# A state-space filter and a gated MLP in one kernel: block 1's signal transform with one split, shift taps on 32-row strips, another home for the third filter's sums, and new instruction orders

## The chip, the cores and the metric

One core of one Trainium2 chip runs the kernel. A core has five engines that run side by side and meet through semaphores: TensorE (PE in the profile, with its weight loads as PEld), VectorE (DVE), ScalarE (ACT), GpSimd (POOL) and SyncE (SP). DMA engines move data; transfers are issued from the queues of SP, POOL and ACT. The metric is the device time in microseconds (us) of one launch.

## What is computed

Batch 1, S = 2048 tokens, D = 640 channels, hidden width F = 1728, bf16 in and out.

```python
x = A_q
# A: gated long convolution, over the normalised x
k_shift = sum over t of k[token - t] * shift_k[:, t]        # 4 taps a channel
kv  = k_shift * v
y   = causal convolution of kv with ssm_k along the tokens  # by FFT of length 2 S
y   = y + kv * ssm_D
h   = x + layernorm(x) * y
# B: gated MLP
g, u = silu(layernorm(h) @ w_gate), layernorm(h) @ w_up
out = h + (g * u) @ w_down
```

## The kernel before

**Blocks.** The tokens are cut into four blocks of N = 512 (i = 0 to 3), and so is the filter ssm_k (m = 0 to 3). Each block of signal and each piece of filter is transformed on TensorE, with tables of cosines and sines (`tab`, `itab`) as the stationary operand; block i of the output is the sum over j of signal j times filter i-j, in the transformed domain, and an inverse transform. `SEQ` at L351 gives the order in which the steps are written down: P product, K third filter, W weights, F feed-forward, S signal, I inverse.

**Transforms.** There are three ways. `fulls` (L593) computes all four quarters of the spectrum by 64 matmuls. `halves` (L574) splits once: 32 matmuls in eight PSUM tiles of four, for the sums over even and over odd positions, then two VectorE operations over 2560 elements (a butterfly: difference and sum). `quads` (L611) splits twice: 16 matmuls in eight tiles of two, then four VectorE operations over 1280 elements and two over 2560. `R4X` (L363) names the blocks whose signal goes by `quads`; the filters go by `halves`. Each PSUM tile of 128 x 640 is copied to SBUF by an eviction (L455), on ScalarE or VectorE.

**The third filter.** `kfwd(2)` (L659) leaves the even half in the first half of K2r and the odd half in the buffer KO. For the filters named in `LO`, VectorE makes the difference (`kb2.0`), and the sum is a DMA that adds KO into K2r (`addto`, L570, issued by POOL; `kb2.1`). `kcomb(2)` (L677) then forms the running sum of filters 1 and 2 in R1, by one VectorE operation over 5120 elements (`kc2.s`, L687). For filters named in `KD` that sum goes by two accumulating DMAs.

**Taps.** `taps(i)` (L699) makes the four-tap shift on TensorE. k is held transposed (channels on partitions); the moving operand is `diag`, the tap weights spread on diagonals of 64 columns, so that two row halves of the array work on 64 channels each. A column group c of 128 channels takes 7 shifts x 2 halves = 14 matmuls (L734) of 64 to 256 columns. For blocks 1 to 3 the tile is evicted into XT (`ke`), and VectorE multiplies it by v (`kv`, L745): three tiles, three evictions and three products a block.

**Order.** No engine's order follows from the program text: `PLAN` (L259) lists, for each engine, the numbers of its tasks in the order in which they run, and the PSUM tile (of four, of two banks each) that each task's result takes. A task waits for the tasks whose data or buffers it needs (L192), so a task that is late holds up all that is listed behind it on its engine. Evictions and some other tasks can run on either of two engines, and the list decides.

**Names that the prediction uses.** `kf`m and `xf`i are the forward matmuls of filter m and signal i, with `e` their evictions, `kt` the transposes of a filter and `kte` their evictions; `kb`, `xb`, `yb` butterflies; `kc` running sums; `p`ji products; `iv`i.j inverse, followed by `e` eviction, `g` product with x, `m` and `s` two statistics passes on ScalarE, `v` and `r` the power -1/2 (r on POOL), `n` normalising; `ht` the DMA transposes of the result; `fg`, `fu` feed-forward matmuls (gate, up), `sg`, `su` their evictions and `mu` their product; `dn` down-projection, `rs` its eviction.

Of the kernel before, what the change touches and what calls it, by code (L numbers as in the profile page):

```python
# [50 lines left out]
class _Graph:  # L51
# [41 lines left out]
    def add(self, name, engs, fn, kind, r=(), w=(), pr=(), pw=(), skip=(), dma=False):  # L93
# [4 lines left out]
        t.opens = None  # L98
# [18 lines left out]
        for pt in pw:  # L117
            if not pt.writers:
                t.opens = pt
# [15 lines left out]
    def arrange(self, plan):  # L135
# [19 lines left out]
        for t in self.order["pe"]:  # L155
            if t.opens is not None:
                prev = last.get(t.opens.unit)
                if prev is not None:
                    t.pre = {x for x in prev.users if x.eng != "pe"}
                    t.deps.update(t.pre)  # L160
                last[t.opens.unit] = t.opens
# [21 lines left out]
    def emit(self, block):  # L183
# [29 lines left out]
        for t in self.glob:  # L213
            kn = known[t.eng]
            fill = self.fills.get(t.name)
            if fill:
                wait_for(t, t.pre | {x for x in t.deps if x.name == fill[0]})
                prog["pe"].append(lambda e, t=t, fill=fill: self.filler(e, t.opens, *fill))
# [50 lines left out]
    "act":  # L269
# [10 lines left out]
    "dve":  # L280
# [10 lines left out]
    "pool":  # L291
        "19 17 15 16 125 165 174 158 192 183 223 225 224 342 396 362 281 371 285 401 380 289 406 389 343 293 420 415 527 466 "
# [18 lines left out]
def bass_sequential_preLN__ssm_conv_h3__swiglu_ffn__prompt_kernel(  # L311
# [917 lines left out]
```

## Time and profile before

| What | Value |
|---|---|
| median of 3 runs | 259.0 us (258.26 to 259.75) |
| profiled execution, first to last instruction | 256.0 us |
| PE busy | 248.5 us (97%), 2253 matmuls |
| PEld busy | 194.7 us (76%) |
| DVE busy | 199.8 us (78%), 256 instructions |
| ACT busy | 184.6 us (72%), 302 instructions |
| POOL busy | 58.6 us (23%), 56 instructions |
| granted TensorE clock | 1.000 |
| moved by DMA | 35.29 MB |

The profiled execution's own time is its span, 256.0 us; the median of the timed runs lies 3.0 us above it, which holds what stands before the first and after the last instruction. The share of a whole span hides stages, so the slices of the page are of more use: the busy tenths of each engine in 40 slices of 6.4 us.

```profile
PE   7999997999999999999999999999999999999995
DVE  3698999999999999999999989999959534111142
ACT  2489999999996895587899789739981854526410
```

PE is busy everywhere, but the ends of its matmuls are modelled, so gaps between issues don't show there. VectorE is full from the third slice to past the middle; ScalarE is full in two stretches, the first of them where the filters and the signal of block 1 are transformed.

### The profile page before, as it was taken

What the parts mean: (1) busy time and instruction counts of PE and PEld (TensorE: products, weight loads), DVE (VectorE), ACT (ScalarE), POOL (GpSimd) and SP (SyncE); (2) the same over time, 40 slices, a digit from 0 to 9 for tenths busy, and PEclk for the clock granted to TensorE, in tenths of its full rate; (3) what the DMA queues carried; (4) which work ended last, traced back from release to release, by engine and by line L of the source; (5) the groups of instructions that cost most, each with busy time, mean ns of one, the idle gap of its engine ahead of it and who ended that gap; (6) DMA issues with size and microseconds to landing.
All of it is one profiled execution on the core that took longest, in us unless ns stands there. A gap on an engine that the chain in (4) does not pass through costs nothing.

```text
span 256.0 us, 5303 instructions
## 1 busy us (share of the span) xinstructions
PE 248.5 (97%) x2253; PEld 194.7 (76%) x2253; DVE 199.8 (78%) x256; ACT 184.6 (72%) x302; POOL 58.6 (23%) x56
## 2 busy tenths in 40 slices
PE   7999997999999999999999999999999999999995
PEld 4767773587888766888887766788886678888763
DVE  3698999999999999999999989999959534111142
ACT  2489999999996895587899789739981854526410
POOL 1001003082312053950030813334130314000000
PEclk9999999999999999999999999999999999999999
DMA  6999946787995049886956036497870142600011
GB/s 224 323 339 208 403 161 134 220 207 192 326 188 95 0 75 126 150 165 168 248 100 109 3 55 139 108 213 139 149 128 0 30 100 43 140 0 3 0 45 57
DMA packets 37620, 35.29 MB, mean 138 GB/s; under 512 B 21203, under 2 KB 32478, under 8 KB 37598
## 3 DMA queue, kind: packets, MB, share of 16 engines
q1 hardware_dynamic: 31792, 23.82, 33.2%
q0 software_dynamic: 5792, 11.14, 25.3%
q8 instruction: 17, 0.28, 0.4%
q14 instruction: 5, 0.04, 0.1%
q10 hardware_dynamic: 14, 0.01, 0.0%
HBM read 16.55 MB, written 2.62 MB: 75 GB/s over the span
## 4 chain that ended last, share of the span: by engine, by line
PE 59%; DVE 32%; DMA 4%; POOL 1%; SPq 1%; issue 1%; ACT 0%; DVEq 0%
PE ps L1032 32%; PE ps L1118 16%; DVE tt L780 9%; DVE Y L780 5%; DMA tab<-cst_tab 4%; PE ps L602 3%; PE ps L922 2%; DVE gu L1053 2%; DVE C L780 2%; DVE XH L637 2%; DVE C L564 2%; PE ps L995 2%; PE ps L622 2%; PE ps L584 2%; POOL mv L840 1%; SPq L450 1%
## 5 line engine op out<-in xcount | busy, mean ns | idle before, releaser
L1118 PE MATMUL ps<-Wd,gu 128*128 128x320 bf16 (+1 forms) x420 | 58.7, 300 | 0.0
L1118 PEld LDWEIGHTS ps<-Wd,gu 128*128 128x128 bf16 (+1 forms) x420 | 38.7, 97 | 18.4 <-issue 3.6
L780 DVE TENSOR_TENSOR tt<-XH,C 128x2560 bf16<-128x2560 bf16 (+1 forms) x31 | 47.8, 1572 | 0.6 <-ACT XH L458 0.6
L1053 DVE TENSOR_TENSOR gu<-gu,ub 128x1024 bf16<-128x1024 bf16 (+1 forms) x32 | 19.9, 621 | 26.4 <-ACT gu L1040 13.8
L1040 ACT ACTIVATE gu<-ps 128x1024 bf16<-128x1024 f32 (+1 forms) x32 | 29.4, 924 | 12.1 <-PE ps L1032 11.9
L1045 ACT ACTIVATE ub<-ps 128x1024 bf16<-128x1024 f32 x24 | 24.6, 1024 | 13.3 <-PE ps L1032 11.4
L1032 PE MATMUL ps<-hnT,GB 128*128 128x256 bf16 x280 | 34.0, 273 | 0.0
L1032 PE MATMUL ps<-hnT,UB 128*128 128x256 bf16 x280 | 33.8, 273 | 0.0
L1032 PEld LDWEIGHTS ps<-hnT,UB 128*128 128x128 bf16 x280 | 27.3, 98 | 3.4 <-ACT KO L458 0.2
L1032 PEld LDWEIGHTS ps<-hnT,GB 128*128 128x128 bf16 x280 | 27.2, 98 | 3.3
L1032 PE MATMUL ps<-hnT,GA 128*128 128x256 bf16 x240 | 28.8, 273 | 0.0
L1032 PE MATMUL ps<-hnT,UA 128*128 128x256 bf16 x240 | 28.5, 273 | 0.1
L840 POOL TENSOR_TENSOR mv<-mv,half 128x1 f32<-128x1 f32 x16 | 21.2, 1328 | 23.9 <-DVE mv L838 23.9
L1032 PEld LDWEIGHTS ps<-hnT,UA 128*128 128x128 bf16 x240 | 23.4, 98 | 3.4 <-ACT C L458 0.5
L1032 PEld LDWEIGHTS ps<-hnT,GA 128*128 128x128 bf16 x240 | 23.4, 98 | 3.2 <-DVE XH L461 0.3
L843 ACT ACTIVATE qo<-xh 128x640 bf16<-128x640 bf16 x28 | 21.0, 750 | 5.8 <-DMA xh<-in_A_q_dram 3.3
L584 PE MATMUL ps<-KT,tab 128*128 128x320 bf16 x128 | 19.8, 300 | 1.8 <-ACT K3r L458 0.7
L937 ACT ACTIVATE qo<-ps,one,st 128x640 bf16<-128x640 f32 x16 | 13.7, 887 | 9.8 <-PE ps L922 9.0
L571 POOL DMA_DIRECT2D xh<-RB x12 | 10.7, 889 | 34.4 <-DVE RB L1135 23.0
L584 PEld LDWEIGHTS ps<-KT,tab 128*128 128x128 bf16 x128 | 11.4, 98 | 8.6 <-ACT K3r L458 1.6
L840 POOL TENSOR_TENSOR st<-st,half 128x4 f32<-128x4 f32 x4 | 8.0, 1988 | 33.3 <-DVE st L835 21.5
L458 ACT ACTIVATE XH<-ps 128x640 bf16<-128x640 f32 x19 | 13.3, 736 | 1.4 <-PE ps L622 0.7
(112 smaller groups left out, 384.3 us busy)
## 6 DMA issues: line engine op xcount, KB each, us to landing
C<-US POOLq DMA_DIRECT2D x6, 640.0 KB, 6.0
kc<-in_A_ssm_k_dram SPq DMA_DIRECT2D x4, 640.0 KB, 10.3
xh<-in_A_q_dram SPq DMA_DIRECT2D x4, 640.0 KB, 5.6
out_dram<-xh SPq DMA_DIRECT2D x15, 160.0 KB, 1.9
kvo<-in_A_v_dram SPq DMA_DIRECT2D x3, 640.0 KB, 4.5
xh<-RB POOLq DMA_DIRECT2D x12, 160.0 KB, 2.9
Wd<-in_B_w_down_dram SPq DMA_DIRECT2D x1, 1280.0 KB, 7.9
C<-K3r POOLq DMA_DIRECT2D x2, 640.0 KB, 8.0
```

Of the source, the lines that this page charges most:

```text
L458: return e.activation(out=dst[1], in_=src(), func=ACTF.Copy, scale=scale)
L571: return g.add(name, "pool", lambda e, n: e.dma_start(dst, src, accum_op=ALU.add, max_dma_last_dim=4096), ("acc", 2 * int(np.prod(dst.shap ...
L584: last = e.matmul(pt.f(c, W), tab[:, f, cs, j], src[:, j, c * W:(c + 1) * W], start=(j == js[0]), stop=(j == js[1]))
L780: g.add(nm, "dve", lambda e, n_: e.tensor_tensor(out=d, in0=a, in1=b, op=op), ("sb", n * D), r=[a, b], w=[d])
L840: g.add(name + "r", "pool", lambda e, n: e.tensor_tensor(out=dst, in0=tmp, in1=hf, op=ALU.pow), ("pp", 4), r=[tmp, half[:]], w=[dst])
L843: g.add(name + "m", "act", lambda e, n: e.activation(out=junk, in_=x, func=ACTF.Identity, scale=-1.0 / D, accum_out=sm), ("aa", D, 0), r=[ ...
L937: g.add(nm + "e", "act", lambda e, n, pt=pt, q2=q2, s=s, j=j: e.activation(out=q2, in_=pt.f2(W), func=ACTF.Identity, scale=s[:, 3, j:j + 1 ...
L1032: last = e.matmul(pt.f(q // 2, 256, o=256 * (q % 2)), w[:, c, f0:f0 + P], hnT[:, c, cols], start=(c == 0), stop=(c == NC5 - 1))
L1040: g.add("sg%d.%d%d" % (i, h, gp), "act", lambda e, n, pa=pa, gv=gv, nf=nf: e.activation(out=gv, in_=pa.f(0, 256 * nf).rearrange("p (f x) - ...
L1045: g.add("su%d.%d%d" % (i, h, gp), "act", lambda e, n, pb=pb: e.activation(out=ub[:].rearrange("p b x -> p (b x)"), in_=pb.f(0, 1024), func ...
L1053: g.add("mu%d.%d%d" % (i, h, gp), "dve", lambda e, n, gv=gv, ubv=ubv: e.tensor_tensor(out=gv, in0=gv, in1=ubv, op=ALU.mult), ("sb", 256 * ...
L1118: last = e.matmul(pt.f(c, W), gu[k, fb, col(i, j)], Wd[k, fb, c * W:(c + 1) * W], start=st, stop=sp)
```

## The change

Seven parts of it act; the rest renames (`BNH` to `BNT`), makes room for choices that are not taken (`KOT`, `DV`, several buffers KO at one address), or lets a matmul task open two PSUM tiles (`opens` becomes a list).

- `R4X` loses block 1: `xfwd(1)` goes by `halves`.
- `KD` gains 2: `kc2.s` becomes two DMAs issued by POOL, `kc2.0` and `kc2.1`.
- `LO` loses ('k', 2): `kb2.1` becomes a VectorE operation over 2560 elements.
- Taps of blocks 1 to 3: column groups 0 to 3 together as one task on four strips of 32 rows, 28 matmuls of 32 to 128 columns for each group, in two PSUM tiles with two evictions (`a`, `b`); the fifth group as before. One product `kv` of 2048 elements takes the place of two of 1024.
- Five evictions early in the kernel run on VectorE that ran on ScalarE (kte2.1, kte3.1, ke1.4, kf2e.010, kf2e.001; kte0.1 in place of kte0.0), and kf0e.011 goes to ScalarE.
- TensorE's order: of block 0's signal one tile, not two, stands ahead of filter 0; all of xf1 and most of filter 3 stand ahead of the first feed-forward task.
- Queues: on SP `itab` stands behind the loads of block 1's x and v, and block 2's v behind the first output; on POOL kc2.0 and kc2.1 stand between iv0.1r and iv0.2r.

The choices:

```diff
     LF = (0, 1, 2, 3)
     SA = ()
     DA = ((1,2),(1,3),(2,3),(3,3))
-    KD = (3,)
+    KD = (2,3)
     DD = (2,)
-    LO = (('k',2),('k',3),('x',3))
+    DV = ()
+    LO = (('k',3),('x',3))
     RD = (0,1,2)
     KS = (1,)
     TS = ((3,3),)
     JP = (0,1)
+    T32 = ((0, 4, 32), (4, 1, 64))
     SEQ = "P01 K W F0 S1 P11 I1 P02 P12 P03 P13 F1 S2 P22 I2 P23 F2 S3 P33 I3 F3"
     HT0 = (0,)
     MB = tuple((a,i) for a in 'kxy' for i in range(4))
     MP = (1,2,3)
     PAIR = True
     BN = (0,)
-    BNH = ()
+    BNT = ()
+    KOT = ()
     DT = ()
     DTA = ()
     HALF = (0, 1, 2, 3)
     R4K = ()
-    R4X = (1,2,3)
+    R4X = (2,3)
     R4Y = (2,3)
 
     Q = N // 2
```

The taps:

```diff
                 return
             ks = kT if i else kT0
             vs = kvo if i else v0
-            for c0 in (0, 2, 4):
-                nc_ = min(2, NC5 - c0)
-                pt = g.tile()
-
-                def mm(e, n, pt=pt, c0=c0, nc_=nc_):
+            for c0, nc_, rr in T32 if i in KVACT else ((0, 2, 64), (2, 2, 64), (4, 1, 64)):
+                nr = P // rr
+                pts = [g.tile() for _ in range(nr // 2)]
+
+                def mm(e, n, pts=pts, c0=c0, nc_=nc_, rr=rr, nr=nr):
                     for b in range(nc_):
                         c = c0 + b
                         for s in (0, 1, 2, 3, -1, -2, -3):
                             j0, j1 = max(0, s), min(3, 3 + s) + 1
                             k0 = 16 + s
-                            for r in range(2):
-                                rows = slice(64 * r, 64 * r + 64)
-                                last = e.matmul(pt.f(r, 64 * (j1 - j0), o=256 * b + 64 * j0), ks[rows, c, k0:k0 + 509:4], diag[rows, c, j0 - s:j1 - s, :],
-                                                start=(s == 0), stop=(s == -3))
+                            for r in range(nr):
+                                rows = slice(rr * r, rr * r + rr)
+                                x0 = rr * r % 64
+                                last = e.matmul(pts[r // 2].f(r % 2, rr * (j1 - j0), o=4 * rr * b + rr * j0), ks[rows, c, k0:k0 + 509:4],
+                                                diag[rows, c, j0 - s:j1 - s, x0:x0 + rr], start=(s == 0), stop=(s == -3),
+                                                **({"tile_position": (rr * r, 0)} if rr < 64 else {}))
                     return last
 
-                g.add("tp%d.%d" % (i, c0), "pe", mm, ("tap64", nc_), r=[diag[:, c0:c0 + nc_], ks[:, c0:c0 + nc_, :]], pw=[pt])
+                g.add("tp%d.%d" % (i, c0), "pe", mm, ("tap%d" % rr, nc_), r=[diag[:, c0:c0 + nc_], ks[:, c0:c0 + nc_, :]], pw=pts)
+                pt = pts[0]
                 cols = slice(c0 * P, (c0 + nc_) * P)
                 d, vv = kvo[:, :, cols], vs[:, :, cols]
                 if i in KVACT:
                     ks_ = XT[i % 2][:, c0:c0 + nc_, :]
-                    evac("ke%d.%d" % (i, c0), (ks_, ks_.rearrange("p b (r y) -> p r b y", r=2)),
-                         lambda pt=pt, nc_=nc_: pt.f2(256 * nc_).rearrange("p r (b y) -> p r b y", b=nc_), N * nc_, pt)
-                    g.add("kv%d.%d" % (i, c0), "dve", lambda e, n, d=d, vv=vv, ks_=ks_: e.tensor_tensor(
-                        out=d.rearrange("p j (b x) -> p b j x", x=64), in0=ks_.rearrange("p b (r j x) -> p (b r) j x", r=2, j=4),
-                        in1=vv.rearrange("p j (b x) -> p b j x", x=64), op=ALU.mult), ("sb", N * nc_), r=[vv, ks_], w=[d])
+                    kr = ks_.rearrange("p b (r y) -> p r b y", r=nr)
+                    for h, pt in enumerate(pts):
+                        kh_ = kr[:, 2 * h:2 * h + 2]
+                        evac("ke%d.%d%s" % (i, c0, "ab"[h] if nr > 2 else ""), (kh_, kh_),
+                             lambda pt=pt, nc_=nc_, rr=rr: pt.f2(4 * rr * nc_).rearrange("p r (b y) -> p r b y", b=nc_), 8 * rr * nc_, pt)
+                    g.add("kv%d.%d" % (i, c0), "dve", lambda e, n, d=d, vv=vv, ks_=ks_, rr=rr, nr=nr: e.tensor_tensor(
+                        out=d.rearrange("p j (b x) -> p b j x", x=rr), in0=ks_.rearrange("p b (r j x) -> p (b r) j x", r=nr, j=4),
+                        in1=vv.rearrange("p j (b x) -> p b j x", x=rr), op=ALU.mult), ("sb", N * nc_), r=[vv, ks_], w=[d])
                     continue
                 for b in range(nc_):
                     cols = slice((c0 + b) * P, (c0 + b + 1) * P)
```

The five lists of `PLAN` are replaced as wholes; of TensorE's the stretch around block 1, in names, before and after:

```diff
- kt3.0 kf1.110 tp1.2 tp1.0 iv0.0 iv0.1 tp1.4 kf2.101 iv0.2 iv0.3 kf3.001 kf2.100 kf2.111
- xf1.30 xf1.31 kf2.010 kf2.001 kf2.011 kf2.110 xf1.11 kf2.000 xf1.10 xf1.01 fu0.00 xf1.20
- xf1.00 fg0.00 xf1.21 fg0.01 kt3.1 kf3.100 fu0.01 kf3.101 kf3.000 kf3.111 kf3.110 kf3.011 kf3.010
+ kf1.010 kt3.0 tp1.0 tp1.4 iv0.0 kf2.101 kf2.010 kf2.000 iv0.1 kf2.111 kt3.1 kf3.100 xf1.111
+ kf2.100 kf2.110 kf2.001 kf2.011 iv0.2 xf1.001 xf1.101 kf3.001 xf1.011 xf1.000 kf3.110 xf1.110
+ xf1.010 iv0.3 xf1.100 kf3.111 kf3.011 kf3.000 fu0.01 kf3.010 fu0.00 fg0.00 kf3.101 fg0.01
```

More of the change, by code (lines that the diff above doesn't have):

```diff
@@ L97, in add @@
         t.pre = set()
-        t.opens = None
+        t.opens = []
         t.tiles = []
@@ L118, in add @@
             if not pt.writers:
-                t.opens = pt
+                t.opens.append(pt)
             else:
@@ L155, in arrange @@
         for t in self.order["pe"]:
-            if t.opens is not None:
-                prev = last.get(t.opens.unit)
+            for pt in t.opens:
+                prev = last.get(pt.unit)
                 if prev is not None:
-                    t.pre = {x for x in prev.users if x.eng != "pe"}
-                    t.deps.update(t.pre)
-                last[t.opens.unit] = t.opens
+                    t.pre |= {x for x in prev.users if x.eng != "pe"}
+                last[pt.unit] = pt
+            t.deps.update(t.pre)
         for t in self.tasks:
@@ L217, in emit @@
                 wait_for(t, t.pre | {x for x in t.deps if x.name == fill[0]})
-                prog["pe"].append(lambda e, t=t, fill=fill: self.filler(e, t.opens, *fill))
+                prog["pe"].append(lambda e, t=t, fill=fill: self.filler(e, t.opens[0], *fill))
             wait_for(t, t.deps)
@@ L411, in bass_sequential_preLN__ssm_conv_h3__swiglu_ffn__prompt_kernel @@
         v0 = sb("v0", 134400, [4, D])
-        KO = sb("KO", 143616, [2, 2, D])
+        KO = [sb("KO%d" % m, 174336 if m in KOT else 143616, [2, 2, D]) for m in range(4)]
         ub = sb("ub", 148736, [2, N])
@@ L660, in kfwd @@
             if m in R4K:
-                quads("kf%d" % m, KT[m], dst, KO, D ** 0.5 / N, m)
+                quads("kf%d" % m, KT[m], dst, KO[m], D ** 0.5 / N, m)
                 return
@@ L665, in kfwd @@
                 return
-            halves("kf%d" % m, KT[m], dst, KO, D ** 0.5 / N, m)
+            halves("kf%d" % m, KT[m], dst, KO[m], D ** 0.5 / N, m)
             if ("k", m) in LO:
-                bfly("kb%d" % m, dst[:, 0:2], KO[:], dst[:, 0:2], dst[:, 2:4], 4 * D, part=1)
-                addto("kb%d.1" % m, dst[:, 0:2], KO[:])
+                bfly("kb%d" % m, dst[:, 0:2], KO[m][:], dst[:, 0:2], dst[:, 2:4], 4 * D, part=1)
+                addto("kb%d.1" % m, dst[:, 0:2], KO[m][:])
                 return
             if ("k", m) in MB:
-                bfly("kb%d" % m, dst[:, 0:2], KO[:], dst[:, 0:2], dst[:, 2:4], 4 * D)
+                bfly("kb%d" % m, dst[:, 0:2], KO[m][:], dst[:, 0:2], dst[:, 2:4], 4 * D)
                 return
             for f in range(2):
-                bfly("kb%d.%d" % (m, f), dst[:, f], KO[:, f], dst[:, f], dst[:, f + 2], 2 * D)
+                bfly("kb%d.%d" % (m, f), dst[:, f], KO[m][:, f], dst[:, f], dst[:, f + 2], 2 * D)
         def kcomb(m, dst, own, prev):
@@ L799, in prod @@
                 op2(nm + ".d", yim, u[:, :, 0], u[:, :, 1], ALU.add, 4)
+                return
+            if (j, i) in DV:
+                x, k, re = XH[j % 2][:], cm[:], tt[:, 1].rearrange("p a b d -> p (a b) d")
+                im = US[:].rearrange("p a b c d -> p (a b) c d")
+                ksw = bass.AP(k.tensor, k.offset + D, [list(k.ap[0]), [2 * D, 4], [-D, 2], [1, D]])
+                nm = "p%d%d" % (j, i)
+                for f2 in range(2):
+                    s = slice(f2, f2 + 3, 2)
+                    op2(nm + ".%da" % f2, t1, x[:, s], k[:, s], ALU.mult, 4)
+                    op2(nm + ".%dc" % f2, re[:, s], t1[:, :, odd], t1[:, :, 1 - odd], ALU.subtract, 2)
+                addto(nm + ".0e", y[:, :, odd], re)
+                op2(nm + ".0b", im, x, ksw, ALU.mult, 8)
+                for q in range(2):
+                    addto(nm + ".%df" % q, y[:, :, 1 - odd], im[:, :, q])
                 return
@@ L969, in inverse @@
                           ("aa", D, 1), r=[x, m[:, 0:1]], w=[q[:], m[:, 1:2]])
-                elif i in BNH:
+                elif (i, j) in BNT:
                     moments(nm, x, j, m[:, 0:2])
@@ L973, in inverse @@
                     stats(nm, x, q[:], m[:, 0:1], m[:, 1:2])
-                rstd(nm, m[:, 1:2], m[:, 3:4], m[:, 2:3], half[:, 0:1], i in BNH or i in SA, D ** -2.0 if i in SA else float(D))
+                rstd(nm, m[:, 1:2], m[:, 3:4], m[:, 2:3], half[:, 0:1], (i, j) in BNT or i in SA, D ** -2.0 if i in SA else float(D))
                 if i in NACT:
@@ L984, in inverse @@
                 g.add(nm + "n", "dve", lambda e, n, x=x, q=q, m=m, mm_=mm_: e.tensor_scalar(
[L985 removed]
+                    out=q[:], in0=x, scalar1=mm_, scalar2=m[:, 3:4], op0=ALU.subtract if (i, j) in BNT or i in SA else ALU.add, op1=ALU.mult),
                       ("ts", D), r=[x, mm_, m[:, 3:4]], w=[q[:]])
```

18 lines of the change are left out of this document (7 added, 11 removed), and 53 rows, old and new, of the table PLAN.

## The prediction

> **What bounds the kernel now.** Read first are the windows: busy time of each engine by stage, in the order PE, PEld, DVE, ACT, POOL.
>
> ```profile
> 31.00:52.00 21.00, 18.92 (x189) 12.19 (x188) 20.59 (x22) 21.00 (x37) 2.38 (x2) 1.00 0.66 191
> 52.00:83.00 31.00, 31.00 (x280) 26.44 (x279) 30.96 (x34) 28.60 (x50) 12.01 (x7) 1.00 0.82 198
> 83.00:113.20 30.20, 29.81 (x287) 22.51 (x285) 29.63 (x35) 22.30 (x38) 14.43 (x12) 1.00 0.63 102
> 113.20:160.00 46.80, 46.53 (x433) 36.91 (x434) 44.99 (x58) 40.47 (x70) 11.24 (x10) 1.00 0.54 117
> ...
> 23.50:113.20 89.70, 87.23 (x813) 66.70 (x811) 88.36 (x94) 79.37 (x133) 29.36 (x22) 1.00 0.74 179
> 39.81:49.22 9.41, 7.34 (x44) 3.03 (x41) 9.03 (x12) 9.41 (x18) 2.38 (x2) 1.00 0.61 130
> ```
>
> From 23.5 to 113.2 us VectorE works 88.36 of 89.70 us: 1.34 us idle. From 31 to 52 ScalarE has no idle time at all, and TensorE the least work. Since a busy PE is modelled, TensorE is read next by counts, in the chain of waits (start, length, what, how many).
>
> ```profile
> 4.09 10.49 DMA tab<-cst_tab
> ...
> 111.64 1.55 DVE kvo L745 x3
> ...
> 113.23 0.72 PE ps L622 x4
> ...
> 121.58 13.10 PE ps L1032 x120
> 134.68 3.77 PE ps L1118 x28
> ...
> 161.37 29.60 PE ps L1032 x270
> ```
>
> A 256-column matmul costs 13.10/120 = 0.109 us, a 320-column one 3.77/28 = 0.135. Over 270 in a row it is still 29.60/270 = 0.110: TensorE runs at its rate, so after 113.23 each matmul more or less moves the end. The chain shows what set 113.23: VectorE's tap product for block 2. The two engines meet there, and I forecast by that meeting point. The timeline of TensorE gives what it lost earlier.
>
> ```profile
> 42.51 0.72 PE L584 MATMUL ps<-KT,tab 128*128 128x320 bf16 x4 [0.69 <-ACT K3r L458]
> ...
> 49.23 2.36 PE L1032 MATMUL ps<-hnT,UA 128*128 128x256 bf16 x20
> ...
> 110.45 2.36 PE L1032 MATMUL ps<-hnT,GB 128*128 128x256 bf16 x20
> ...
> 138.29 2.44 PE L734 MATMUL ps<-diag,kT 64*128 64x256 bf16 x70
> 140.67 0.72 PE L1032 MATMUL ps<-hnT,GB 128*128 128x256 bf16 x5
> ```
>
> From 39.81 to 49.22 it issued 42 matmuls (44 with two still ending), 42 x 0.135 = 5.7 us of work in 9.4: 3.7 us lost to ScalarE's evictions. At 110.45 its last work before the meeting point begins and is issued by 110.45 + 20 x 0.109 = 112.63, so there it lost 0.6.
>
> **The change, part by part.** Prices, by group (the mean in ns stands after the busy time):
>
> ```profile
> L637 DVE TENSOR_TENSOR XH<-XH,OS 128x1280 bf16<-128x1280 bf16 x6 | 4.8, 820 | 0.0
> L564 DVE TENSOR_TENSOR C<-C,KO 128x2560 bf16<-128x2560 bf16 x5 | 7.4, 1490 | 0.5 <-ACT KO L458 0.5
> L687 DVE TENSOR_TENSOR C<-C,C 128x5120 bf16<-128x5120 bf16 x1 | 2.8, 2822 | 0.0
> L745 DVE TENSOR_TENSOR kvo<-XT,kvo 128x1024 bf16<-128x1024 bf16 x6 | 3.9, 685 | 0.0
> L460 DVE COPY KT<-ps 128x1280 bf16<-128x1280 bf16 x1 | 0.8, 815 | 0.0
> L460 DVE COPY kT<-ps 128x512 bf16<-128x512 bf16 x1 | 0.7, 692 | 0.1
> L461 DVE TENSOR_SCALAR KO<-ps 128x640 bf16<-128x640 f32 x1 | 0.8, 825 | 0.4 <-PE ps L584 0.4
> L780 DVE TENSOR_TENSOR C<-tt 128x2560 bf16<-128x2560 bf16 x1 | 1.5, 1485 | 0.0
> L984 DVE TENSOR_SCALAR qo<-xh,mv 128x640 bf16<-128x640 bf16 x16 | 7.1, 444 | 2.7 <-POOL mv L840 2.7
> L1053 DVE TENSOR_TENSOR gu<-gu,ub 128x1024 bf16<-128x1024 bf16 x24 | 16.5, 688 | 23.1 <-ACT gu L1040 13.8 <-ACT ub L1045 9.3
> L571 POOL DMA_DIRECT2D C<-K3r x2 | 2.9, 1446 | 5.3 <-DMA K3r<-KO 5.3
> ```
>
> and two rows of the transfers (KB each, us from issue to landing):
>
> ```profile
> C<-K3r POOLq DMA_DIRECT2D x2, 640.0 KB, 8.0
> ...
> itab<-cst_itab SPq DMA_DIRECT2D x1, 512.0 KB, 6.6
> ```
>
> *Block 1's transform.* On VectorE the four quarter-size operations go, 4 x 0.82 = 3.28 us; two of 2560 elements stay. TensorE gets 16 more 320-column matmuls, 16 x 0.135 = 2.2 us. I cost them at nothing: the new order puts all of them before the first feed-forward matmul, in the stretch where 3.7 us were lost to ScalarE, whose evictions stay eight of 640. Without that cover they cost 2.2.
>
> *Third filter.* The running sum kc2.s leaves VectorE (-2.82), the butterfly sum kb2.1 comes (+1.49). POOL issues two transfers instead of one, 1.45 us each; behind them stands iv0.2's power (iv0.2r), whose input comes, by VectorE's new order, two products of 5120 elements (2 x 2.8) later than the transfers' own. They land some 8 us on; the products that read the sum stand 29 VectorE operations behind. I cost this at nothing; without cover iv0.2r is 2 x 1.45 = 2.9 us late. One wait is new: kb2.1 reads KO on VectorE, so ScalarE's eviction kf3e.110 into KO waits for VectorE, where it waited for a transfer. Both come near 50 us in the sums below; if VectorE is later, ScalarE's stream shifts with it, and that is rival B's price.
>
> *Tap products.* One of 2048 elements for two of 1024. Between 0.685 (1024) and 1.490 (2560) the slope is 0.52 ns an element, so an estimate of 1.22 for 1.37: -0.15 a block.
>
> *Taps on 32 rows.* Four of five column groups take 28 matmuls each instead of 14. Before, 70 take 140.67 - 138.29 = 2.38 us, 34 ns each. The rows of the tap line, and a window of 0.03 us at its start:
>
> ```profile
> L734 PE MATMUL ps<-diag,kT x70: 189/216/277, 138.3 to 140.5; 64*128 64x192 bf16 x20, 64*128 64x128 bf16 x20, 64*128 64x64 bf16 x20, 64*128 64x256 bf16 x10
> 138.28:138.31 0.03, 0.02 (x2) 0.01 (x2) 1.00 0.00 0
> ```
>
> Columns are 20 x 192 + 20 x 128 + 20 x 64 + 10 x 256 = 10240; at 109/256 = 0.43 ns each that is 4.4 us in a row, and 2.38 were taken: the two row halves run side by side, and the window shows both started. Four strips at once would halve 4/5 of 2.2: -0.87 us a block. The other end is the old mean spacing, 112 x 0.034 = 3.8 for 1.9: +1.9. The rows are nearer the first; I take -0.6. The Trainium skill speaks against this part: TensorEngine Tiling (Array Packing), section Instruction Overhead, gives each matmul about 60 cycles whatever its columns, and warns against a tiling factor from a dimension that is already small; TensorE: Matmul & The Clock Gate, section "Wait — 56ns, not 53.3ns?", puts start-to-start at no less than about 25 ns. The trace agrees only in part: the window has two starts in 0.03 us, so no such floor stands between row halves. By 25 ns for each of 112 the part would cost 2.8 us for 1.9.
>
> *Order, start.* The timeline of VectorE before the first product:
>
> ```profile
> 14.55 0.82 DVE L461 TENSOR_SCALAR KO<-ps 128x640 bf16<-128x640 f32 x1 [0.41 <-PE ps L584]
> ...
> 19.77 1.49 DVE L564 TENSOR_TENSOR C<-C,KO 128x2560 bf16<-128x2560 bf16 x1 [0.54 <-ACT KO L458]
> ...
> 23.50 1.49 DVE L780 TENSOR_TENSOR tt<-XH,C 128x2560 bf16<-128x2560 bf16 x1 [0.26 <-ACT XH L458]
> ```
>
> The eviction goes to ScalarE; filter 0's tiles now stand before most of the signal's, and the tiles that need the late half of tab (landing 4.09 + 10.49 = 14.6) stand fifth, so the three waits should go: 0.82 + 0.41 + 0.54 + 0.26 = 2.0 us earlier (bounds 0 and 2.0). On SP's queue two loads are moved behind a wait. itab stands behind block 1's v, which waits for the last xf0 matmul; its reader iv0.0 has kf1 (32 x 0.135 = 4.3), taps (1.8) and 30 transposes ahead of it on TensorE, just over the 6.6 us of its landing: nothing, or up to 1 us on iv0.0 and all of ScalarE behind it. Block 2's v stands behind the first output; three down-projections (84 x 0.135 = 11.3 us) cover it.
>
> *Order, VectorE's evictions.* kte2.1, kte3.1, ke1.4 and two of kf2 come over: 2 x 0.815 + 0.69 + 2 x 0.825 = +3.97. Ahead of block 2's tap product now stand p03.d and iv1.3n, mu1.00 behind it: 1.485 + 0.444 - 0.688 = +1.24.
>
> *VectorE's sum to the meeting point.* -3.28 - 2.82 + 1.49 - 0.30 + 3.97 + 1.24 = +0.30; start -2.0; of the 1.34 us idle I let half go (bounds: all gone, or doubled): -0.7. Together -2.4: 113.2 becomes 110.8. Bounds: 113.2 - 2.0 + 0.3 - 1.34 = 110.2 and 113.2 + 0.3 + 1.34 = 114.8.
>
> *TensorE's sum to it.* It needs ScalarE's stream:
>
> ```profile
> 33.87 2.05 ACT L458 ACTIVATE XT<-ps 128x1024 bf16<-128x1024 f32 x2
> ...
> 40.96 0.82 ACT L845 ACTIVATE qo<-xh,mv 128x640 bf16<-128x640 bf16 x1
> ...
> 47.21 1.37 ACT L458 ACTIVATE KO<-ps 128x640 bf16<-128x640 f32 x2
> 48.38 0.80 ACT L458 ACTIVATE C<-ps 128x640 bf16<-128x640 f32 x1
> ...
> 52.25 1.15 ACT L1045 ACTIVATE ub<-ps 128x1024 bf16<-128x1024 f32 x1
> ```
>
> An eviction takes (48.38 - 47.21)/2 = 0.585, a statistics pass 0.82. Between block 1's first tap eviction (33.87) and su0.00 (52.25) the new order has six evictions and two passes more and half a tap eviction (about 0.5) less: 18.4 + 3.5 + 1.6 - 0.5 = 23.0, so su0.00 at 56.9. fu0.01 can start when the four PSUM tiles let it, three evictions and four passes before (5.0): 51.9, against 49.23, 2.7 later. But 26 matmuls of 320 columns that followed then (all of xf1, nearly all of kf3) are done by now: -3.5. With tap 2 at -0.6 TensorE is ready at 112.63 + 2.7 - 3.5 - 0.6 = 111.2, bounds 109 (no loss to ScalarE) and 116.
>
> The later of both is 111.2, 2.0 earlier than 113.23. Behind it the same matmuls follow, with block 3's taps 0.6 shorter: -2.6. The span of 256.0 becomes 253.4. The median of the runs, 259.0, lies 3.0 above the profiled span; the same beside the new one: **256.4 us**.
>
> **Rivals.**
> *A, taps bound by issue (slower).* Excess e a block moves the meeting point to 111.8 + 2e (taps 1 and 2) and the rest by e; the gain is used up at 3e = 1.4, e = 0.47, or (1.9 + 0.47)/112 = 21 ns a matmul; from there this decides. At 34 ns (e = 1.9): 115.6 - 113.2 + 1.9 = +4.3, 263.3. Halfway between the two, e = 1.2, it is +2.2: 261.2, which stands for A. For it: twice the instructions for the same columns. Against: the two starts in the window.
> The Trainium skill's floor of about 25 ns (TensorE: Matmul & The Clock Gate, "Wait — 56ns, not 53.3ns?") would be such a spacing: e = 0.9, +1.3, 260.3.
> *B, ScalarE holds the feed-forward back.* If the four tiles do not let fu0.01 run ahead and it waits for su0.00's turn, TensorE comes up to 5 us later; at half, 113.7 - 113.2 - 0.6 = -0.1: 258.9. For it: ScalarE's 21.00 of 21.00. Against: the new order spaces these tiles four deep.
> *C, VectorE waits for the evictions it now takes over or for ScalarE's.* Idle doubled and half the start lost: 113.2 + 0.3 + 1.34 - 1.0 = 113.8, less 0.6: 259.0. For it: it had only 1.34 idle before, so each cover is thin.
> *D, the change moves work but not the meeting point* (start waits return as others): 113.2 kept, -0.6: 258.4.
>
> **How the numbers follow.** Forecast 0.61, A 0.15, B 0.10, C 0.08, D 0.06. About 0.5% (1.3 us) is what a measurement here can tell from no change. Faster, below 257.7: the forecast and a little of B, 0.63; slower, above 260.3: A and a part of B and C, 0.17; the rest, 0.20, is the same. All bounds at their good end give 110.2 at the meeting point and -0.87 after: -3.9, 255.1; one more microsecond for what follows unseen, 254.0. Up, the range takes in B, C, D and A as far as e = 0.9 (3 x 0.9 - 1.4 = +1.3): 260.4. The likeliest case alone: 254.0 to 257.7.
>
> **What would show it.** The taps of block 3 at about 1.8 us for 126 matmuls (over 2.7: A). First product of VectorE near 21.5; first feed-forward matmul near 52, with xf1 and most of kf3 before it (B: 55 or later); block 2's first xf2 matmul near 111; VectorE's idle time before it under 1.4 us. The forecast is wrong if xf2 starts after 113, or if TensorE has gaps behind it.

## The result, and the profile after

| | before | after |
|---|---|---|
| median of 6 runs each, us | 258.91 (258.08 to 259.75) | 255.47 (254.98 to 256.05) |
| ratio | | 0.9884, 95% interval 0.9858 to 0.9909 |
| profiled execution, first to last instruction, us | 256.0 | 253.2 |
| PE busy, matmuls | 248.5 us, 2253 | 247.6 us, 2437 |
| DVE busy | 199.8 us | 196.5 us |

The kernel became 1.2% faster, some 3.0 us (0.9 to 1.4%). The forecast was 256.4 us, from a span of 253.4.

The windows of the kernel after (us, then busy time and instructions of PE, PEld, DVE, ACT, POOL, the granted clock, the DMA share and GB/s), over nearly the stretches that were shown of before:

```profile
31.00:52.00 21.00, 20.54 (x269) 14.16 (x268) 20.56 (x24) 20.90 (x34) 6.82 (x4) 1.00 1.05 261
52.00:83.00 31.00, 31.00 (x271) 25.82 (x270) 30.96 (x33) 27.45 (x49) 9.24 (x8) 1.00 0.80 160
83.00:113.20 30.20, 30.04 (x359) 23.51 (x357) 30.13 (x34) 21.96 (x38) 13.86 (x11) 1.00 0.77 143
113.20:160.00 46.80, 46.73 (x498) 36.79 (x496) 44.73 (x61) 40.77 (x73) 13.83 (x11) 1.00 0.47 101
...
21.50:110.50 89.00, 88.54 (x958) 68.75 (x956) 88.04 (x96) 77.47 (x129) 29.92 (x21) 1.00 0.87 194
```

Between 31 and 52 us TensorE now has 269 matmuls where it had 189 (56 of the 80 more are the smaller matmuls of the strips, 126 for 70), and ScalarE is as full as it was (20.90 of 21.00). VectorE's idle time up to its meeting with TensorE is 89.00 - 88.04 = 0.96 us (1.34 before).

The meeting itself is the start of block 2's signal transform ("xf2" below), which needs VectorE's tap product for block 2 and the end of TensorE's earlier work. In VectorE's timeline, from its first product of a signal with a filter ("first product" below) on, and in TensorE's (start, length, what, and in brackets the idle time ahead with what ended it):

```profile
21.88 1.49 DVE L783 TENSOR_TENSOR tt<-XH,C 128x2560 bf16<-128x2560 bf16 x1
...
108.76 1.48 DVE L783 TENSOR_TENSOR C<-tt 128x2560 bf16<-128x2560 bf16 x1
110.16 1.22 DVE L748 TENSOR_TENSOR kvo<-XT,kvo 128x2048 bf16<-128x2048 bf16 x1
```

```profile
52.23 1.26 PE L1049 MATMUL ps<-hnT,UA 128*128 128x256 bf16 x10
...
108.94 2.35 PE L1049 MATMUL ps<-hnT,GA 128*128 128x256 bf16 x20
111.44 0.72 PE L619 MATMUL ps<-kvo,tab 128*128 128x320 bf16 x4 [0.16 <-DVE kvo L748]
```

The first product starts at 21.88 (23.50 before), without a wait. TensorE's last work ahead of the meeting is issued by 108.94 + 20 x 0.109 = 111.12, VectorE's tap product ends at 110.16 + 1.22 = 111.38: the two come within 0.3 us of each other, VectorE last, and xf2 starts at 111.44 (113.23 before). From first product to xf2 it was 113.23 - 23.50 = 89.73 us and is 111.44 - 21.88 = 89.56: what was gained ahead of the meeting, 1.79 us, is all but 0.17 the earlier start. The size of the start is that of one profile against one; over all the kernels of this document, the first product begins at 21.88 to 22.86 in the ten profiles with the new start, and at 23.50 to 24.35 in the four with the old one.

Behind the meeting, the chain of waits (start, length, what, count):

```profile
48.66 1.40 DVE C L561
50.06 2.74 DVE Y L783
...
132.30 0.45 PE ps L732 x14
132.75 8.29 PE ps L1049 x75
141.04 1.24 PE ps L732 x104
142.28 3.88 PE ps L1135 x28
...
158.59 29.51 PE ps L1049 x270
...
250.53 0.55 DVE xh L1018
```

Block 3's taps take 0.45 us for the fifth group (14 matmuls on two row halves) and 1.24 for the other four (112 on four strips; the chain counts 104 records of them): 1.69 us, where 2.38 were taken. The 270 feed-forward matmuls behind cost what they did, 29.51 against 29.60. The chain of before ended with

```profile
253.41 0.55 DVE xh L1001
```

so from xf2 to this last piece it was 253.41 - 113.23 = 140.2 us, and is 250.53 - 111.44 = 139.1. Of this 1.1 us the taps are 0.69.

### The profile page after: what moved, and what is told of

It is laid out like the page before. It is cut to its first block, busy times and chain, and to the rows that moved or that the text cites. A ratio compares the mean times of both kernels' runs of the same rounds, so it can differ in the third digit from the quotient of the medians.

```text
span 253.2 us, 5660 instructions
## 1 busy us (share of the span) xinstructions
PE 247.6 (98%) x2437; PEld 194.9 (77%) x2437; DVE 196.5 (78%) x251; ACT 182.6 (72%) x300; POOL 60.9 (24%) x57
## 4 chain that ended last, share of the span: by engine, by line
PE 58%; DVE 34%; DMA 3%; issue 2%; POOL 2%; ACT 1%; SPq 0%; DVEq 0%
PE ps L1049 32%; PE ps L1135 15%; DVE tt L783 10%; DVE Y L783 6%; PE ps L599 4%; DMA v<-in_A_v_dram 3%; PE ps L581 2%; DVE C L561 2%; DVE C L783 2%; PE ps L1012 2%; DVE gu L1070 2%; PE ps L939 1%; DVE xh L961 1%; DVE kvo L748 1%; DVE US L783 1%
## 5 line engine op out<-in xcount | busy, mean ns | idle before, releaser
L857 POOL TENSOR_TENSOR mv<-mv,half 128x1 f32<-128x1 f32 x16 | 20.3, 1271 | 43.7 <-DVE mv L855 43.7
L581 PEld LDWEIGHTS ps<-KT,tab 128*128 128x128 bf16 x128 | 12.1, 98 | 6.0 <-DVE mv L855 0.5
L857 POOL TENSOR_TENSOR st<-st,half 128x4 f32<-128x4 f32 x4 | 9.9, 2478 | 23.8 <-DVE st L852 17.4
```

The costliest lines, as they stand in the source:

```text
L581: last = e.matmul(pt.f(c, W), tab[:, f, cs, j], src[:, j, c * W:(c + 1) * W], start=(j == js[0]), stop=(j == js[1]))
L857: g.add(name + "r", "pool", lambda e, n: e.tensor_tensor(out=dst, in0=tmp, in1=hf, op=ALU.pow), ("pp", 4), r=[tmp, half[:]], w=[dst])
```

## The experiments

The theory: the gain is the earlier start and the third set of taps; the other parts trade work between three engines that are all nearly full, and each pays for itself only with the others and with the order. The rivals were, from part to part, that a part has no effect, and that the price is another than the one named. All old parts together in the new orders were not run. "First product to xf2" is read from each profile; since the first product's own start differs by up to 1 us between profiles of kernels that are the same up to there (21.88 to 22.86), this column says more on a change behind it than the span does. Ratios and intervals are to the kernel before, run beside each group: its median was 258.91 beside the kernel after and 258.26 to 258.65 beside the others, so between rows the ratios compare better than the medians.

| kernel | median, us | ratio (95%) | span | first product to xf2 |
|---|---|---|---|---|
| after | 255.47 | 0.9884 (0.9858 to 0.9909) | 253.2 | 89.56 |
| taps on 64 rows | 257.07 | 0.9942 (0.9916 to 0.9969) | 254.3 | 89.76 |
| block 1 split twice | 260.35 | 1.0070 (1.0043 to 1.0097) | 258.4 | 94.01 |
| running sum on VectorE | 258.61 | 1.0013 (0.9991 to 1.0035) | 256.1 | 92.23 |
| butterfly sum by transfer | 260.95 | 1.0110 (1.0073 to 1.0146) | 258.6 | 94.80 |
| five evictions on ScalarE | 258.97 | 1.0029 (1.0009 to 1.0049) | 256.8 | 92.86 |
| start in the old order | 257.40 | 0.9950 (0.9931 to 0.9970) | 255.3 | 89.18 |
| more VectorE work | 257.12 | 0.9956 (0.9938 to 0.9974) | 255.2 | 90.93 |
| more TensorE work | 256.97 | 0.9941 (0.9919 to 0.9963) | 254.7 | 90.53 |
| more of both | 257.24 | 0.9941 (0.9916 to 0.9966) | 255.3 | 90.75 |
| tap product one place ahead | 255.95 | 0.9894 (0.9867 to 0.9922) | 253.8 | 89.23 |
| new parts, old orders | 264.23 | 1.0199 (1.0158 to 1.0241) | 261.9 | 95.28 |
| the same, running sum on VectorE | 258.59 | 0.9987 (0.9956 to 1.0018) | 256.5 | 90.17 |

### Taps on 64 rows again

```diff
-    T32 = ((0, 4, 32), (4, 1, 64))
+    T32 = ((0, 2, 64), (2, 2, 64), (4, 1, 64))
```

The six tasks and products stand at the places of the new ones.

> The changed kernel with the taps of blocks 1 to 3 on 64-row halves again (three tasks, three evictions and three products a block, in the places of the new order). Theory 'meeting point' (the end is set by the later of VectorE's tap product of block 2 and TensorE's own queue, which come to within 0.3 us of each other near 111.4, and by TensorE alone after it): a block's taps take 2.4 instead of 1.7 us; TensorE comes to the meeting point 0.7 to 1.4 later and block 3's taps add 0.7 behind it: +1.1 to +1.8, time 256.6 to 257.3. Rival 'taps bound by issue': the strips gain nothing, 255.5. Rival 'VectorE's chain alone sets the meeting point': only block 3's share, 256.2.

257.07, in the theory's range; by the ratios it is 1.5 us above after. The profile bears out less of it: of the 1.1 us of span 0.38 lie ahead of the first product, where the edit changes nothing, 0.20 between it and xf2, and 0.5 behind. TensorE is ready 0.47 us later, counted from the first product, and not 0.7 to 1.4, so this run alone does not part the theory from its second rival (256.2). The chain of waits of this kernel shows block 3's taps:

```profile
132.88 0.45 PE ps L703 x14
...
141.62 1.94 PE ps L703 x56
```

0.45 + 1.94 = 2.39 us again, against 1.69. On four strips the matmuls start 1.24/112 = 0.011 us apart, a third of the 34 ns they had on two row halves; a spacing of 21 ns or more, from which the part would have lost, is ruled out.

### Block 1 split twice again

```diff
-    R4X = (2,3)
+    R4X = (1,2,3)
```

> The changed kernel with block 1's signal split twice again (16 matmuls fewer, four VectorE operations of 0.82 more), its tiles in the places of the new order. 'Meeting point': VectorE comes 2.9 later to 114.3, TensorE's 2.2 us less lie where ScalarE holds it anyway: +2.9, time 258.4. Rival 'TensorE's work alone counts' (its matmuls fill 98% of the span): -2.2, time 253.3. Rival 'order alone': 255.5.

The direction is the theory's, the size is not: 260.35, 2 us above the expectation. VectorE's rows in the timeline:

```profile
67.95 1.49 DVE L532 TENSOR_TENSOR K3r<-K3r,KO 128x2560 bf16<-128x2560 bf16 x1
69.36 1.49 DVE L754 TENSOR_TENSOR tt<-XH,C 128x2560 bf16<-128x2560 bf16 x1
70.76 1.56 DVE L754 TENSOR_TENSOR tt<-tt 128x1280 bf16<-128x1280 bf16 x2
72.23 0.69 DVE L1041 TENSOR_TENSOR gu<-gu,ub 128x1024 bf16<-128x1024 bf16 x1
```

and ScalarE's and TensorE's after them:

```profile
72.95 1.02 ACT L1033 ACTIVATE ub<-ps 128x1024 bf16<-128x1024 f32 x1 [0.91 <-DVE gu L1041]
```

```profile
68.46 2.35 PE L1020 MATMUL ps<-hnT,GA 128*128 128x256 bf16 x20
74.03 2.31 PE L1020 MATMUL ps<-hnT,UA 128*128 128x256 bf16 x10 [3.22 <-ACT ub L1033]
76.13 1.82 PE L1020 MATMUL ps<-hnT,UB 128*128 128x256 bf16 x10
```

VectorE's extra 3.28 us make the product g x u of block 0's feed-forward late; that product holds the buffer ub, ScalarE cannot evict into it, the PSUM tile stays taken, and TensorE waits 3.22 us. So the engines do not first meet at block 2's tap product: they are tied together here, 40 us earlier. And the matmuls after the wait are slow: ten take 2.10 us (74.03 to 76.13) where ten took 1.09. The windows give the reason:

```profile
70.00:76.00 6.00, 2.78 (x18) 1.89 (x16) 5.97 (x7) 5.03 (x9) 2.31 (x3) 0.82 1.06 234
76.00:80.00 4.00, 4.00 (x33) 3.34 (x32) 4.00 (x6) 3.19 (x8) 2.17 (x2) 0.84 1.07 191
```

The granted clock is 0.82 and 0.84 there. That is 6 x 0.18 + 4 x 0.16 = 1.7 us of clock, most of the 2 us that the expectation lacked. The executions of this kernel bear it out: four of the twelve show a mean clock of 0.999 or 1.000 and took 259.01 to 259.39 us, the other eight show 0.987 to 0.993 and took 260.17 to 262.12.

In the kernel after, ScalarE's eviction into ub at 69.29 waits 0.26 us for the same product, and TensorE's next feed-forward group, at 70.37, has no wait in its row: the tie holds there too, just without cost.

### The running sum on VectorE

```diff
-    KD = (2,3)
+    KD = (3,)
-dve: .. p11.0a kb3.0 ..     pool: .. iv0.1r kc2.0 kc2.1 iv0.2r ..
+dve: .. p11.0a kc2.s kb3.0 ..     pool: .. iv0.1r iv0.2r ..
```

> The changed kernel with the third filter's running sum back on VectorE as one operation over 5120 elements, just ahead of kb3.0; the butterfly sum stays on VectorE. 'Meeting point': VectorE 2.7 later, +2.7, time 258.2. Rival 'TensorE's work alone': 255.5.

258.61, near the theory's 258.2 (five of the twelve executions, with a mean clock of 0.999 or 1.000, took 257.77 to 258.23; the other seven, at 0.993, took 258.52 to 259.69). TensorE's timeline shows the same place, with a shorter wait:

```profile
73.33 1.26 PE L1020 MATMUL ps<-hnT,UA 128*128 128x256 bf16 x10 [2.64 <-ACT ub L1033]
74.44 1.25 PE L1020 MATMUL ps<-hnT,UB 128*128 128x256 bf16 x10
```

Ten matmuls take 74.44 - 73.33 = 1.11 us right after it: no loss of clock behind this one in the profiled execution.

### The butterfly sum by transfer

```diff
-    LO = (('k',3),('x',3))
+    LO = (('k',2),('k',3),('x',3))
-dve: .. kb2.0 kb2.1 ..     pool: .. iv0.1r kc2.0 kc2.1 ..
+dve: .. kb2.0 ..     pool: .. iv0.1r kb2.1 kc2.0 kc2.1 ..
```

> The changed kernel with the third filter's butterfly sum by a transfer again (ahead of the two transfers of the running sum on POOL). 'Meeting point': VectorE saves 1.4, but the buffer KO is held until the transfer lands, some 6 us after VectorE's difference; ScalarE's kf3e.110 and all behind it wait about 5 us, the feed-forward begins near 57 instead of 52, TensorE comes to the meeting point near 116: time 259 to 260.5. Rival 'VectorE's chain alone': -1.4, time 254.1. Rival 'TensorE's work alone': 255.5.

260.95, just over the range. ScalarE's eviction into KO waits for the transfer, and TensorE for the eviction:

```profile
54.43 0.70 ACT L426 ACTIVATE KO<-ps 128x640 bf16<-128x640 f32 x1 [4.60 <-DMA C<-KO]
```

```profile
55.19 2.02 PE L552 MATMUL ps<-KT,tab 128*128 128x320 bf16 x8 [4.15 <-ACT KO L426]
57.00 2.26 PE L1020 MATMUL ps<-hnT,UA 128*128 128x256 bf16 x10
```

In the kernel after, that eviction starts at 50.10, straight behind kb2.1 (48.66 + 1.40 in the chain above). The first feed-forward matmul stands at 57.00, 4.8 us later.

### Five evictions on ScalarE

```diff
-dve: .. kte2.1 .. ke1.4 .. kf2e.010 .. kte3.1 .. kf2e.001 ..
+act: kte2.1 behind kte2.0, ke1.4 behind ke1.0b, kf2e.010 behind kf2e.101, kte3.1 behind kf2e.111, kf2e.001 behind kf2e.110
```

> The changed kernel with the five evictions kte2.1, ke1.4, kf2e.010, kte3.1 and kf2e.001 on ScalarE again, each where its tile is made. Theory 'balance' (ScalarE's stream of block 1's and the filters' evictions sets when the feed-forward begins; VectorE and TensorE then meet, first through the buffer ub in block 0's feed-forward, then at block 2's tap product): ScalarE's stream grows by 2 x 1.1 + 0.5 + 2 x 0.6 = 3.9, the first feed-forward matmul comes near 56 instead of 52, TensorE at the meeting point near 114.5, although VectorE has 4.0 less to do: +2.5 to +3.5, time 258 to 259. Rival 'VectorE's chain alone': its 4.0 us less show as a gain, under 254. Rival 'TensorE's work alone': 255.5.

258.97. VectorE has five evictions less, 3.97 us by their rows, and the meeting still comes 3.3 us later: the first feed-forward matmul stands at 56.23 (52.23 after), because ScalarE sets it, busy for 24.00 of the 24.00 us between 33 and 57. In that stretch VectorE's time is the cheaper one.

### The start in the old order

```diff
-pe: .. kt0.1 xf0.00 kf0.011 .. kf0.110 xf0.01 ..     act: .. xf0e.00 kf0e.011 kf0e.001 ..
+pe: .. kt0.1 xf0.01 xf0.00 kf0.011 .. kf0.110 ..     act: .. xf0e.01 xf0e.00 kf0e.001 ..
+dve: .. la0.0b1 kf0e.011 la0.0a ..
```

> The changed kernel with the start of the kernel before: xf0.01 ahead of xf0.00 and filter 0, kf0e.011 evicted by VectorE; all else as changed. 'Balance': VectorE's first product comes 1.6 later (23.5 instead of 21.9), and it has been full ever since: its chain to the meeting point shifts by 1.6 less what idle time of it swallows (0.4 at 26.9, about 1 at 44.5), ScalarE and TensorE follow it: +0.5 to +1.6, time 256 to 257.1. Rival 'TensorE's work alone': 255.5 (only 0.4 of a wait for tab).

257.40, a little over the range (by the ratios 1.7 us above after). The first product starts at 24.35, 2.5 us later, and xf2 at 113.53, 2.1 later, as is the end: what the start loses is hardly made up behind it. The kernel before, with that order, has its first product at 23.50, so 0.85 of the 2.5 us is scatter or has another cause.

### More work for one engine, for the other, for both

VectorE: the product p12.1a (1.4 us) twice. TensorE: seven matmuls of 512 columns that nothing reads, ahead of fg1.00.

```diff
                 op2(nm + "a", t1, x, k, ALU.mult, 4)
+                if nm == "p12.1":
+                    op2(nm + "a2", t1, x, k, ALU.mult, 4)
```

```diff
-    "fills": {'wb0': ['zmem', 3], 'k0t4.0': ['zmem', 1]},
+    "fills": {'wb0': ['zmem', 3], 'k0t4.0': ['zmem', 1], 'fg1.00': ['tab0', 7]},
```

> The changed kernel with one VectorE operation of 2560 elements (p12.1a, 1.4 us) done twice, between block 0's feed-forward and block 2's tap product; nothing else is changed. 'Balance': block 2's tap product ends 1.4 later at 112.8, TensorE waits for it: +1.35, time 256.8. Rival 'TensorE's work alone': 255.5.

> The changed kernel with seven idle matmuls of 512 columns (7 x 0.216 = 1.5 us) ahead of fg1.00, TensorE's last task before block 2's transform; VectorE has nothing more to do. 'Balance': TensorE comes to the meeting point at 112.6 instead of 111.1, VectorE at 111.4 as before: +1.2, time 256.7. Rival 'VectorE's chain alone sets the meeting point' (as the chain of waits tells it): 255.5.

> Both at once: p12.1a twice and the seven idle matmuls ahead of fg1.00. 'Balance': the two lie beside each other, the later of 112.8 and 112.6 counts: +1.4, time 256.9. Rival 'they add' (one follows the other in a chain): +2.7, time 258.2.

257.12, 256.97 and 257.24. From first product to xf2 the three are 1.4, 1.0 and 1.2 us longer than after. Either engine alone moves the meeting by most of what it gets, and both together by no more than one: it is the later of two sums, and the sums are nearly equal. The medians lie some 0.3 above the expectations.

### The tap product one place ahead

```diff
-dve: .. p03.d kv2.0 ..
+dve: .. kv2.0 p03.d ..
```

> The changed kernel with block 2's tap product (kv2.0) ahead of p03.d on VectorE. 'Balance': VectorE is ready at 110.0, but TensorE not before 111.1: -0.3, which can't be told from 255.5. Rival 'VectorE's chain alone sets the meeting point': -1.4, time 254.1.

255.95, no difference from after that the intervals can tell. VectorE's side of the meeting is 1.4 us earlier on paper, but kv2.0 then waits 0.63 us for its eviction, and xf2 starts when TensorE is ready: its row has no wait ahead of it. VectorE alone can give nothing more here.

### New parts, old orders

Every engine's list of before, its tasks put one for one into the new names: the transform by halves in the tiles of the old one, the strip taps in the place of the two old groups, kb2.1 behind kb2.0 on VectorE, kc2.0 and kc2.1 in kb2.1's place on POOL.

> All parts of the change (block 1 by one split, strips of 32 rows, the third filter's sums) in the orders, tiles and engines of the kernel before: the new tasks stand where their forerunners stood, kb2.1 behind kb2.0, the two transfers of the running sum where kb2.1's transfer stood. 'Balance': VectorE has 4.9 us less to do up to the meeting point, so TensorE alone sets it: 112.63, plus 0.8 for the six matmuls of xf1 that now lie among the feed-forward ones, less 0.7 for block 2's taps and some 0.5 of its wait: 112.2 to 112.8, then block 3's taps -0.7: -1.1 to -1.7 against the kernel before, 256.6 to 257.2. Rival 'the parts alone made the gain': 255.5. Rival 'the order alone made it': 258.3.

This was a miss: 264.23 where 256.6 to 257.2 were expected, slower than before by 2%. TensorE's timeline and SP's:

```profile
64.35 2.36 PE L1020 MATMUL ps<-hnT,UB 128*128 128x256 bf16 x20
70.12 2.29 PE L1020 MATMUL ps<-hnT,GA 128*128 128x256 bf16 x10 [3.41 <-DMA hnT<-qo]
72.21 1.79 PE L1020 MATMUL ps<-hnT,GB 128*128 128x256 bf16 x10
```

```profile
58.53 0.37 SPq L418 DMA_DIRECT2D Wd<-in_B_w_down_dram  x1
58.94 7.15 SPq L421 DMA_TRANSPOSE hnT<-qo  x2
```

POOL's timeline, and the landings of the transposes issued from 57 us on:

```profile
54.27 2.65 POOL L539 DMA_DIRECT2D C<-C  x2 [10.84 <-DVE C L532]
```

```profile
DMA to landing us min/median/max: 5.4/7.9/10.4
```

The last two transposes of block 0's normalised output take 5.4 and 10.4 us, and TensorE waits 3.41 us for them. POOL issued the running sum's two transfers, 640 KB each, not 5 us ahead of them, and SP a load of w_down just ahead. In the kernel after, the same two views have

```profile
50.38 2.65 POOL L568 DMA_DIRECT2D C<-C  x2 [2.60 <-DVE C L561]
```

```profile
DMA to landing us min/median/max: 2.7/2.8/2.9
```

The sum goes out 3.9 us sooner, and the transposes land in under 3 us. But the load of w_down stands behind the transposes there (at 62.47 on SP's queue), so this pair alone does not part the sum's transfers from the load; the next run does.

### The same, with the running sum on VectorE

```diff
-    KD = (2,3)
+    KD = (3,)
-dve: .. xb1.1 kb3.0 ..     pool: .. kc2.0 kc2.1 ..
+dve: .. xb1.1 kc2.s kb3.0 ..
```

> The new parts in the old orders as before (264.2 us), but the third filter's running sum by VectorE, ahead of kb3.0, where VectorE had 3.61 us idle; the two transfers of 640 KB go. Theory: those transfers, issued at 54.27 and 55.16, shared the DMA engines with block 0's last two transposes, which landed at 69.36 and 70.03 (62.54 and 63.75 before the change); TensorE then waited 3.41 us and ran at a lower clock for some 1.7 us' worth. Without them the transposes land by 65, the wait and the lost clock go: 5.1 us off, less up to 1 of VectorE's 2.82 that its idle time does not cover: 259.1 to 260.3. Rival 1: it is the load of w_down issued just ahead of the transposes that delays them: still above 67, and 263.5 to 264.5. Rival 2: the old orders of the evictions cost the time by themselves: the transposes land early, and the time is still above 262.

258.59, 0.5 us below the theory's range and far from both rivals. The w_down load still stands ahead of the transposes. SP's timeline, the landings, and the timelines of VectorE and TensorE:

```profile
58.18 0.37 SPq L418 DMA_DIRECT2D Wd<-in_B_w_down_dram  x1
58.59 2.95 SPq L421 DMA_TRANSPOSE hnT<-qo  x2
```

```profile
DMA to landing us min/median/max: 4.0/4.5/5.1
```

```profile
61.49 2.81 DVE L655 TENSOR_TENSOR C<-C,C 128x5120 bf16<-128x5120 bf16 x1
65.17 1.49 DVE L532 TENSOR_TENSOR K3r<-K3r,KO 128x2560 bf16<-128x2560 bf16 x1 [0.87 <-ACT KO L426]
```

```profile
66.19 1.25 PE L1020 MATMUL ps<-hnT,GA 128*128 128x256 bf16 x10
```

The transposes land in 4.0 to 5.1 us, and TensorE's wait of 3.41 us is gone; the sum itself costs VectorE nothing, since all of its 2.81 us lie in idle time, of which 0.87 is left. So the sum by transfers was what made the old orders slow, by 5.4 us of span, 1.7 of it clock (last section); where VectorE has no idle time, as in the new orders, the same sum on VectorE costs 2.9. With the load still ahead, the transposes take 1.3 to 2.2 us longer than in the kernel after; whether that is the load's doing was not tried. The run also shows that the new parts, with the sum in the better of the two places tried, gain nothing in the old orders: 0.9987, with one in the interval.

## Why the prediction was right, step by step

**The size.** The span was 253.2 against 253.4. The time came out 0.9 below 256.4, and that is one term: the 3.0 us that the prediction put around the span. The profiled execution of after took 255.3 with a span of 253.2, 2.1 around it; the other five runs, with spans of 252.9 to 253.9, took the same 2.1 more. The 3.0 was the distance from one profiled span to the median of other executions, so it held their scatter too; in the later runs of the kernel before it is 1.9 to 3.1, mostly near 2.0.

That the span itself came out so near is in part luck, since two smaller misses cancel: xf2 starts at 111.44, 0.24 later than the 111.2 forecast, and the stretch behind it is 1.1 us shorter instead of 0.6. And the engine that comes last to the meeting is the other one: the forecast had VectorE ready at 110.8 and TensorE at 111.2, and measured it is VectorE, by 0.26.

**Start: -2.0 forecast, -1.62 measured** (21.88). The three waits are gone, and no wait stands ahead of the first product. The old order of the start alone costs 2.1 us of span, 1.7 us by the ratios.

**VectorE's sum: 110.8 forecast, 111.38 measured.** Two terms fell short: the start by 0.4, and the idle time let go, 0.38 (1.34 to 0.96) instead of 0.7. The estimate of 1.22 us for a tap product of 2048 elements is the row's own 1.22.

**TensorE's sum: 111.2 forecast, 111.12 measured**, with its middle steps: su0.00 at 56.9 forecast and 57.35 measured, the first feed-forward matmul at 51.9 and 52.23. That ScalarE's stream sets this place was argued from full windows; the five evictions put back on ScalarE show it.

**Block 1's halving at nothing.** Its 16 more matmuls did find their cover: TensorE reaches the meeting as forecast. What the prediction did not see is what the 3.28 us on VectorE were worth: put back, they cost 5.2 us of span, since VectorE's lateness reaches TensorE through ub in block 0's feed-forward, and the clock falls. So the path it reckoned by, with block 2's tap product as the first place where the two engines meet, was incomplete: each engine's sum took every part together, but the sums were compared at the later meeting only. That the earlier one costs nothing in the kernel after (0.26 us of ScalarE's time, and no wait in TensorE's row) was not worked out, and is luck.

**The third filter's sums at nothing.** Right for the order that runs, and the cover named (the products that read the sum stand far behind) holds: no VectorE operation of the kernel after waits for these transfers. It was incomplete: the transfers need more than a late reader. They run beside block 0's transposes when issued 4 us later, in the old orders, and cost 5.4 us there. The new wait of kf3e.110 on VectorE came where it was put, at 50.10, and costs nothing there.

**Taps: -0.6 forecast, -0.69 measured** for block 3. Rival A is out: the spacing is 11 ns, well below the 21 from which it decides. The floor of about 25 ns between starts (the Trainium skill, TensorE: Matmul & The Clock Gate, "Wait — 56ns, not 53.3ns?") does not hold across strips of rows that run side by side; by it, as an estimate, the 112 would have taken 2.8 us, and they took 1.24.

**Rivals B, C and D.** The first feed-forward matmul at 52.23 rules out B (55 or later), 0.96 us of idle time C, xf2 at 111.44 D. B does come about with the five evictions back on ScalarE (56.23). The prices of the parts undone one by one, in span: 1.1 (taps) + 5.2 (halves) + 2.9 and 5.4 (running sum on VectorE and butterfly sum by transfer) + 3.6 (evictions) + 2.1 (start) add up to 20.3 us, seven times the whole gain of 2.8 (two of them, 5.2 and the 5.4 of the butterfly sum, hold 1.7 us of lost clock each). They are prices of a broken balance, not shares of the gain.

**Open.** The 0.4 us behind the meeting that the taps don't account for were not followed up. Nor was the fifth tap group on 32 rows tried: by the kernel's text it needs two PSUM tiles instead of one.

## What to carry to other kernels

Where several engines are nearly full, cost a change as one sum for each engine up to the point where they meet, the start included, and take the later; look for an earlier place where one holds up the other through a buffer. Parts tried one by one say what breaks the balance, not what each part brings. Before a sum goes from an engine to a transfer, look at which transfers run beside it at that time, not only at when its result is read. And look for idle time on the engine first: the same operation cost nothing in a gap and 2.9 us without one.

## What the runs showed of the hardware

The price of a wait of TensorE can jump. In the profiled executions the granted clock fell behind the waits of 3.22, 4.15 and 3.41 us, and behind the one of 2.64 it did not. The windows right behind them are, in this order, those shown above of block 1 split twice (0.82 and 0.84), and of the butterfly sum by transfer, of the new parts in the old orders, and of the running sum on VectorE:

```profile
56.00:60.00 4.00, 4.00 (x24) 2.88 (x24) 3.92 (x4) 3.97 (x10) 1.64 (x2) 0.62 0.96 168
```

```profile
70.00:74.00 4.00, 3.88 (x22) 2.85 (x23) 2.45 (x4) 3.82 (x7) 0.00 (x0) 0.59 1.04 304
```

```profile
70.00:76.00 6.00, 3.36 (x32) 2.78 (x30) 5.97 (x7) 3.71 (x6) 2.42 (x3) 1.00 0.90 160
```

That is 4 x 0.38 = 1.5 and 4 x 0.41 = 1.6 us of clock in these windows, on top of the wait. In windows of 1 us the same traces show what the means hide: the clock stands at 0.50 for three whole windows (74 to 77 us with block 1 split twice, 56 to 59 and 70 to 73 in the other two), in parts of the windows on either side, and is back at 1.00 after that. With these parts each of the three lost 1.7 us, so by this sum the clock was at half for about 3.4 us each time. The Trainium skill (TensorE: Matmul & The Clock Gate, "Part 1: The HAM clock gate") has the clock go down to half after an idle window of about 3.4 us. The traces agree on the half. Counted from the last matmul's issue (68.46 + 20 x 0.109 = 70.64, to 74.03) the idle time of block 1 split twice was 3.4 us, at the edge of that window.

A length of wait from which the clock falls is not shown. Four of the twelve executions of the kernel with the wait of 3.22 us kept their clock, and seven of the twelve with the wait of 2.64 show a mean of 0.993, which is what one such stretch would make of a span of 256 us (an estimate: 1.7/256 = 0.007). Those were not profiled, so whether they lost it behind this wait stays open. All six executions of the kernel after show 1.000.
